# Where one weight tile's conversion stands at the end of the first block, and where the next batch's loads stand in the load queue

## Chip, cores and metric

The kernel runs on one core of a Trainium2 chip. Its time is the device time of one execution in microseconds; several executions are timed, and the median is given. One more execution was recorded by the hardware profiler: the profile and the trace are of that one.

## What is computed

Two stages follow each other. The first is a linear attention for 8 batches of 8 heads, each with 576 rows of 64 values: `kv = k^T v`, `out = q kv`, then each row of `out` is divided by its root mean square and multiplied by `g_norm`. The result is laid out as x, 4608 rows (tokens) of 512. The second stage is `h = x w_in` (512 to 2048), `g = max(0.01 h, h)`, and the output `g w_out` (2048 to 512), in float32. The two weights arrive as 64-bit floats and are converted to 32-bit in the kernel.

```python
def _attn_ref(q, k, v, g_norm):
    kv = np.einsum('bhsd,bhse->bhde', k, v)
    out = np.einsum('bhsd,bhde->bhse', q, kv)
    rms = np.sqrt(np.mean(out * out, axis=-1, keepdims=True) + 1e-06)
    return (out / rms * g_norm).astype(np.float32)

def _moe_ref(x, w_in, w_out):
    h = x @ w_in
    g = np.maximum(0.01 * h, h)
    return (g @ w_out).astype(np.float32)
```

## The kernel before

**Blocks and units.** The 4608 tokens are cut into nine blocks of 512. Block 0 is computed in the ordinary way by `first_block` with three of the four chunks of the weights, while the rest of the weights is still on its way. Block 1, the remainder of block 0 and the other blocks then run in the main loop, by a scheme of seven products in place of eight (Strassen's, in Winograd's form): `product_h` makes h, `product_o` makes the output. Blocks 2 and later use the scheme twice over for h (`product_h_two`). A unit is one chunk of one block. Units are numbered by `now`; each has seven slots `t`, one per product, and `at = 7 * now + t` counts slots from the start of the main loop. The output's products of a unit follow two slots behind its h (`LAG`).

**Converting a weight tile.** A tile is 128 x 512 values, and there are 32. `round_f64` converts one with two steps on ScalarE (ACT: `add` L264 and `cut` L262, reading the raw 64-bit tile), one on VectorE (DVE, L266), one on ACT (L271), and two on VectorE (L281, L284). `round_w(j)` begins tile j: it does L264, L262 and L266. `finish_w()` does the other three of a tile that was begun. The raw tiles share a few buffers, so the load of tile 28 waits until tile 25's two first ACT steps have read theirs.

**Block 0.** `first_block` runs n from 0 to 12. Step n makes one piece of h (eight h_ps matmul records), lets ACT turn it into g (L1143), and then makes the output products of the piece before it (eight o_acc records), which need that g. `between(n, 0)` is called ahead of these output products and `between(n, 1)` behind them. What they do stands in `plan`: a number begins that tile, `f` finishes the one begun, `a` and `t` do a step of the attention for batch 1 or the rest of batch 0, and `x` makes the sums of x for block 1. The last lines are

```python
(8, 1): (21, f, a), (9, 0): (a, a, a, a, a, a, 22, f), (9, 1): (x, 23),
(10, 0): (f, 24), (10, 1): (f, 25), (11, 0): (f,)}
```

At n = 11 the last piece of h is made, and at n = 12 its output products. Behind them ACT (L1156) and VectorE (L1158) copy the block's four sums out of PSUM. In this part of the program each engine's order is the order in which the code issues instructions (`pin`).

**The first slots of block 1.** `product_h` works in pairs of PSUM banks (h_a and h_c, then h_b and h_d). The products go into the banks in the order h_a, h_c, h_a, h_c, h_a, h_c, h_a; each is read by ACT (`copy`, L938, L940, L945) or added by VectorE (L698) before the next one goes into the same bank.

**Sums of weights.** POOL (GpSimd) makes sums and differences of weight quarters for the products of the scheme, and `combine` makes more, in the buffer `stage`, for the double scheme. `put_off` and `write_later` write them to DRAM some slots later (L735, in the profile w<-w_all, w<-stage and w<-pairs), so that `stage` can be used again; from slot 26 on `read` (L822, w_all<-w) fetches them in the order of use. POOL also makes sums of g (`gs`) for the output's products, and sums of x in `stage` for block 2.

**Loads of the attention's inputs.** `to_load` is a list of small load jobs: the k and v tiles of a pair of heads (two transfers, L138) or its q tile (four transfers, L168). The attention's steps append to it, and one job is taken at the end of each slot:

```python
load_some(2 if at in (19, 20) else 1)
```

All of these, the writes and the reads are issued by one engine, SP, in the order of the code. Output stores are issued by ACT (L1114). Each transfer of SP and ACT increments one of eight completion semaphores, taken in turn by the scheduler, and is preceded by a wait for the last transfer that used that semaphore.

Of the kernel before, what the change touches and what calls it, by code (L numbers as in the profile page):

```python
# [24 lines left out]
def kernel(  # L25
# [121 lines left out]
    def load_some(n=1):  # L147

        while to_load and n > 0:
            b, p, what = to_load.popleft()  # L150
            load_pair(b, p, what)
            n -= 1

    def load_pair(b, p, what="kvq", homes=None):


        if "k" in what:
            for i, (to, src) in enumerate(((k_ins, k), (v_ins, v))):
                to[b, p] = load_two(nc.sync, src[b, 2 * p:2 * p + 2],
                                    homes[i] if homes else in_tile("kv"[i]))  # L160
        if "q" not in what:
            return
        t = homes[2] if homes else ins.tile([P, T * D], F32, tag="q_in", name="q_in")
        for l in range(2):
            for c in range(2):
                r0, n = 64 * l + 32 * c, T * D - 32 * c
                src = q[b, 2 * p + half_of(p, l)].rearrange("(t s) d -> t (s d)", s=T)
                pin(nc.sync.dma_start(t[r0:r0 + 32, :n], src[:, 32 * c:]))  # L168
        q_ins[b, p] = t
# [132 lines left out]
    def load_w(j, *eng):  # L302
        eng = eng or (nc.sync,)
        dst, src = w_jobs[j]
        if w_in.dtype == I64:
            w_raws[j] = load_f64(src.bitcast(U32), eng)
        else:
            load(dst, src, eng)

    def rounding(j, high_first=False):  # L310
        if w_in.dtype == I64:
            yield from round_f64(w_jobs[j][0], w_raws.pop(j), high_first)
# [418 lines left out]
    def write_later():  # L731
        for item in list(later):
            item[0] -= 1
            if item[0] < 0:
                pin(nc.sync.dma_start(*item[1:]))  # L735
                later.remove(item)
# [81 lines left out]
    def read(to):  # L818
        nonlocal n_read
        while n_read < min(to, len(reads)):  # L820
            c, k = reads[n_read]
            pin(nc.sync.dma_start(w_place(n_read), w1_dram[c][:, SLOT[k], :, :]))  # L822
            n_read += 1
# [140 lines left out]
    def inner_w2(c):  # L964
        y = w2_sb[1][c]
        t1, t2, t3, t4 = (w2_sb[0][c][:, u, N2 + s * P:N2 + s * P + P]
                          for u in range(2) for s in range(2))
        y11, y12, y21, y22 = (y[:, u, s * P:s * P + P] for u in range(2) for s in range(2))
        add(nc.gpsimd, t1, y12, y11, True)
        add(nc.gpsimd, t2, y22, t1, True)  # L970
        add(nc.gpsimd, t3, y22, y12, True)
        add(nc.gpsimd, t4, y21, t2, True)

    def inner_g(n, half):

        g = g_of(n)[3]
        a11, a21, a12, a22 = (g[:, n, :] for n in range(4))
        s1, s2, s3, s4 = (gi[:, n, :] for n in range(4))
        if half == 0:
            add(nc.gpsimd, s1, a21, a22)  # L980
            add(nc.gpsimd, s2, s1, a11, True)
        else:
            add(nc.gpsimd, s3, a11, a21, True)
            add(nc.gpsimd, s4, a12, s2, True)
# [115 lines left out]
    def go(steps, n=None):  # L1100
        while n is None or n > 0:
            if next(steps, steps) is steps:
                return
            n = None if n is None else n - 1
# [13 lines left out]
    def load_part(os, key):  # L1118

        os[key] = opool.tile([P, 2, N2], F32, tag="o", name=f"o{key}", bufs=6)  # L1120
        r0, c0 = ((int(d) - 1) * N2 for d in key)
        pin(nc.sync.dma_start(
            os[key], part_dram[r0:r0 + N2, c0:c0 + N2].rearrange("(t p) m -> p t m", p=P)))

    def first_block(between):
# [27 lines left out]
        for t in range(4):  # L1153
# [9 lines left out]
    t, a, f, x = "tafx"  # L1163
# [2 lines left out]
            (5, 0): (13, f, a), (5, 1): (14, f), (6, 0): (15, f), (6, 1): (16, f),  # L1166
            (7, 0): (a, a, 17, f), (7, 1): (a, 18, f), (8, 0): (19, f, a, 20, f),
            (8, 1): (21, f, a), (9, 0): (a, a, a, a, a, a, 22, f), (9, 1): (x, 23),
            (10, 0): (f, 24), (10, 1): (f, 25), (11, 0): (f,)}
    loaded, x_sides = 12, None  # L1170

    def between(n, half):
# [56 lines left out]
    def go_o():  # L1229
        while o_queue:  # L1230
            if next(o_queue[0], o_queue) is not o_queue:
                return True
            o_queue.popleft()
# [3 lines left out]
    for i, chunks in rounds:  # L1237
# [7 lines left out]
        for c in chunks:  # L1245
# [5 lines left out]
            for t in range(7):  # L1251
                slot = 7 * c + t
                go(h_steps, 1)
                if not one:

                    if t == 6:
                        go(h_steps, 1)
                    if slot in LATE_SLOTS:
                        go(late, 1)
                    for _ in range(FINE_SLOTS.get(slot, 0)):  # L1260
                        go(a_steps, 1)
                    if i + 1 < NB:
                        if slot == 20:
                            x_sides, new_quarters, sums, inner = sides_x(i + 1)
                        if slot in (20, 21, 22):
                            go(sums, 2 if slot == 20 else 1)
                        if slot == 24:
                            inner(0)
                        elif slot == 25:
                            inner(1)  # L1270
                    load_some()

                if now - 1 in seconds:
                    for half in range(2):
                        if t == (6 if half else 4):
                            inner_g(now - 1, half)
                    if t == 5 and now - 1 < 2 * NC + NC - K:
                        inner_w2(units[now - 1][1])
                if (7 * now + t == 7 * NC + 4):
                    while writes:  # L1280
                        pin(nc.sync.dma_start(*writes.pop()))
                if slot in HELD and i == NB - 1:
                    pass
                elif waited == LAG:
                    go_o()
                elif o_queue:
                    waited += 1
                write_later()
                at = 7 * now + t
                for key in PARTS.get(at, ()):  # L1290
                    if at == 33:
                        part_os = os
                    load_part(part_os, key)
                if at in READS:
                    read(READS[at])
                if one:
                    if not rest and rounded < len(w_jobs):
                        steps = rounding(rounded)
                        rest.extend((3, 3, 1))
                        rounded += 1  # L1300
                    if rest:
                        go(steps, rest.popleft())
                    if loaded < min(rounded + 2, len(w_jobs)):
                        load_w(loaded)
                        loaded += 1
                    for chunk, only in DIRECT.get(at, ()):
                        go(combine(chunk, 2, only=only))
                    if at == 18:
                        direct_0 = combine(0, 2, nc.vector)
                    if at in (18, 19, 22, 23):  # L1310
                        go(direct_0, 1)
                    if t == 3 and nxt[0] < 2 and nxt[1] != c:
                        h_sides, more_h = sides_w1(nxt[1])
                        if now == 0:
                            go(combine(0, 1))
                    if t == 5 and nxt[0] < 2 and nxt[1] != c:
                        more_h()
                    if t == 0 and units[now - 1][1] != c and now > 0:
                        for part in range(2):
                            go(combine(c, part))  # L1320
                    if at in (15, 16):
                        load_pair(2, at - 15)
                    go(late, LATE_ONE.get(at, 0))
                    go(a_steps, A_SLOTS.get(at, 0))
                    load_some(2 if at in (19, 20) else 1)
                    if at == 7 * NC - 4:
                        x_sides, _, sums, _ = sides_x(0)
                    elif at == 7 * N1 - 4:
                        x_sides, new_quarters, sums, inner = sides_x(2)
                    if at in (7 * NC - 4, 7 * NC - 3, 7 * N1 - 4, 7 * N1 - 3):  # L1330
                        go(sums, 2)
                    if at == 7 * N1 - 3:
                        inner(0)
                    elif at == 7 * N1 - 2:
                        inner(1)
# [44 lines left out]
```

## Time and profile before

| | us |
|---|---|
| median of 3 runs | 923.47 (921.96 to 923.55) |
| profiled execution, its own time | 920.04 |
| its span in the profile | 918.3 |
| TensorE (PE) busy in the span | 906.4 |
| VectorE (DVE) busy | 621.1 |
| ScalarE (ACT) busy | 346.9 |
| GpSimd (POOL) busy | 391.0 |
| the profile's mean DMA rate | 220 GB/s |

Times in the profile are microseconds from the start of the span. Between the span and the execution's time lie 1.7 us. The three timed runs lie 1.9 to 3.5 us above the profiled execution. In a timeline a row gives start, duration, engine, line and operation, output and inputs by name, shape, and in brackets the time that the engine was idle just before and what ended that. L126 and L698 are helpers for matmuls and for additions, so their rows are told apart by the tiles. PE is TensorE's matmul, PEld its weight load, SPq the queue of SP.

### The profile page before, as it was taken

The numbers are of one execution on the slowest core, as the hardware profiler recorded it, in microseconds if no ns is written. First come the engines' busy times: TensorE is split into PE (matmuls) and PEld (weight loads), VectorE is DVE, ScalarE is ACT, GpSimd is POOL, SyncE is SP. The second block draws the span as 40 slices with busy tenths as digits, with TensorE's granted clock in tenths as the row PEclk, the third lists the DMA queues.
The fourth block names the chain that finished last, engine by engine and source line by source line (L and its number), as shares of the span: only waits on it lengthen the run. The fifth ranks groups of instructions, "written<-read, shape, count | busy, mean of one in ns | idle before, by whom it ended". The sixth has DMA issues, their size and how long they took to land.

```text
span 918.3 us, 18139 instructions
## 1 busy us (share of the span) xinstructions
PE 906.4 (99%) x7024; PEld 783.8 (85%) x7024; DVE 621.1 (68%) x1127; ACT 346.9 (38%) x679; POOL 391.0 (43%) x467
## 2 busy tenths in 40 slices
PE   8999899999999999999999999999999999999998
PEld 4544388878898999899999999999999999999997
DVE  5765855767556876687756876578669755755565
ACT  5756464132235233433243334332443333223330
POOL 2000479969633473226421642264226522542222
PEclk9999999999999999999999999999999999999999
DMA  8998175897989778777886788758765676666633
GB/s 261 223 270 210 60 242 172 231 307 220 340 280 317 222 226 260 232 234 216 247 261 218 233 247 268 224 168 207 251 180 175 188 221 199 181 194 218 200 108 92
DMA packets 92405, 202.16 MB, mean 220 GB/s; under 512 B 10016, under 2 KB 44448, under 8 KB 92320
## 3 DMA queue, kind: packets, MB, share of 16 engines
q1 hardware_dynamic: 81344, 189.14, 69.3%
q10 hardware_dynamic: 10528, 10.69, 3.5%
q8 instruction: 56, 0.92, 0.4%
q0 software_dynamic: 448, 1.18, 0.3%
q14 instruction: 29, 0.24, 0.1%
HBM read 173.44 MB, written 27.53 MB: 219 GB/s over the span
## 4 chain that ended last, share of the span: by engine, by line
PE 88%; DVE 4%; DMA 3%; ACT 2%; issue 1%; SPq 1%; POOL 1%; DVEq 0%; ACTq 0%; POOLq 0%
PE o_c L126 18%; PE o_a L126 18%; PE h_ha L126 11%; PE h_hb L126 10%; PE h_hc L126 8%; PE h_hd L126 8%; PE h_ps L126 3%; PE o_acc L126 3%; PE o_ps L126 3%; PE h_a L126 1%; PE h_c L126 1%; DMA pairs<-in_v_dram 1%; PE kv_ps L126 1%; PE h_b L126 1%; DMA w_all<-w 1%
## 5 line engine op out<-in xcount | busy, mean ns | idle before, releaser
L698 POOL TENSOR_TENSOR gs<-g 128x512 f32<-128x512 f32 x66 | 84.8, 1285 | 249.1 <-ACT g L913 249.1
L913 ACT ACTIVATE g<-g 128x512 f32<-128x512 f32 x127 | 80.1, 631 | 146.4 <-DVE g L698 146.3
L1032 ACT COPY w_all<-h_ha 128x512 f32<-128x512 f32 x84 | 48.9, 582 | 170.6 <-PE h_ha L126 158.3
L126 PE MATMUL o_c<-pairs,gs 128*128 128x256 f32 x392 | 93.2, 381 | 0.0
L126 PE MATMUL o_a<-pairs,gs 128*128 128x256 f32 x392 | 93.0, 380 | 0.0
L698 DVE TENSOR_TENSOR o<-h_hb,o 128x128 f32<-128x128 f32 x104 | 29.8, 286 | 83.4 <-ACT pairs L1032 83.3
L126 PEld LDWEIGHTS o_c<-pairs,gs 128*128 128x128 f32 x392 | 71.3, 190 | 9.5 <-POOL pairs L698 1.2
L126 PEld LDWEIGHTS o_a<-pairs,gs 128*128 128x128 f32 x392 | 71.3, 190 | 8.1
L698 DVE TENSOR_TENSOR o<-o_a,o 128x512 f32<-128x512 f32 (+1 forms) x93 | 62.5, 672 | 23.0 <-PE o_a L126 22.5
L698 DVE TENSOR_TENSOR o<-o_c,o 128x512 f32<-128x512 f32 x80 | 54.7, 683 | 26.0 <-PE o_c L126 25.7
L126 PE MATMUL h_ha<-stage,w_all 128*128 128x128 f32 x448 | 59.9, 276 | 0.9 <-POOL stage L698 0.9
L126 PEld LDWEIGHTS h_ha<-stage,w_all 128*128 128x128 f32 x448 | 56.7, 192 | 4.0 <-POOL stage L698 1.1
L698 DVE TENSOR_TENSOR g<-g,pairs 128x512 f32<-128x512 f32 x84 | 55.6, 689 | 1.9
L698 POOL TENSOR_TENSOR pairs<-g 128x128 f32<-128x128 f32 x52 | 23.7, 456 | 77.0 <-PE h_hb L126 48.4
L698 DVE TENSOR_TENSOR w_all<-h_hc,w_all 128x512 f32<-128x512 f32 x56 | 38.3, 684 | 15.8 <-PE h_hc L126 15.8
L698 DVE TENSOR_TENSOR o<-h_hd,o 128x128 f32<-128x128 f32 x78 | 22.1, 283 | 38.1 <-ACT pairs L1032 38.0
L126 PE MATMUL o_acc<-w,g 128*128 128x512 f32 x96 | 43.8, 598 | 3.6 <-ACT g L1143 3.6
L126 PE MATMUL h_hb<-stage,w_all 128*128 128x128 f32 x336 | 46.7, 275 | 0.0
L698 POOL TENSOR_TENSOR gs<-gs,g 128x512 f32<-128x512 f32 x33 | 44.7, 1355 | 2.6
L698 POOL TENSOR_TENSOR gs<-g,gs 128x512 f32<-128x512 f32 x33 | 45.4, 1377 | 0.0
L1032 ACT COPY pairs<-h_hb 128x384 f32<-128x384 f32 x84 | 40.0, 476 | 13.7 <-PE h_hb L126 13.3
L126 PE MATMUL h_hb<-xT,w_all 128*128 128x128 f32 x224 | 43.3, 275 | 0.0
(240 smaller groups left out, 2240.8 us busy)
## 6 DMA issues: line engine op xcount, KB each, us to landing
w_all<-w SPq DMA_DIRECT2D x196, 448.0 KB, 4.2
pairs<-w SPq DMA_DIRECT2D x56, 512.0 KB, 4.4
out_dram<-o ACTq DMA_DIRECT2D x35, 256.0 KB, 4.9
v_in<-in_v_dram SPq DMA_DIRECT2D x27, 288.0 KB, 4.4
k_in<-in_k_dram SPq DMA_DIRECT2D x26, 288.0 KB, 4.2
q_in<-in_q_dram SPq DMA_DIRECT2D x52, 144.0 KB, 5.7
q_in<-in_q_dram SPq DMA_DIRECT2D x52, 140.0 KB, 5.7
w<-stage SPq DMA_DIRECT2D x12, 512.0 KB, 4.1
```

What stands on the lines that cost most here:

```text
L126: pin(nc.tensor.matmul(*args, **kw))
L698: ins = eng.tensor_tensor(out_, a, b_, op=ALU.subtract if minus else ALU.add)
L913: first_turn(nc.scalar.activation(t, t if src is None else src, func=AF.Prelu, alpha=SLOPE))
L1032: nc.scalar.copy(q[:, at], bank)
```

## The change

Two places change. In `plan`, tile 24 is still begun ahead of the output products of step 10, but it is finished, and tile 25 begun, one place later: ahead of the output products of step 11, and so behind L1143 of the last piece of h. Tile 25 is finished behind the output products of step 12, the last ones. In the main loop, two load jobs in place of one are taken at slots 24 and 25.

```diff
-            (10, 0): (f, 24), (10, 1): (f, 25), (11, 0): (f,)}
+            (10, 0): (f, 24), (11, 0): (f, 25), (12, 1): (f,)}
...
-                    load_some(2 if at in (19, 20) else 1)
+                    load_some(2 if at in (19, 20, 24, 25) else 1)
```

In the built program the instructions of PE, DVE and POOL stand in the same order as before. On ACT the last L1143 moves ahead of three steps: L271 of tile 24 and L264 and L262 of tile 25. On SP the order before, from slot 24, was: q of pair 0 of batch 3; three writes of w_0; k and v of pair 0; two reads of w_0; q of pair 1; ten writes of w_1 and w_3; k and v of pair 1; a write of w_3_0 from `pairs`; reads and writes as they follow. After the change it is: q, k and v of pair 0; the three writes of w_0; q, k and v of pair 1; the two reads of w_0; the ten writes; the write from `pairs`; then as before. The last of the ten writes, w_3 from `stage`, now stands where v of pair 1 stood.

## The prediction

> **What bounds the kernel now.** I read the page first (busy times, the 40 slices), then TensorE's waits, then the timelines of PE, ACT and DVE around the first edit and of SP and POOL around the second, and last the chain that ended last.
>
> ```profile
> PE 906.4 (99%) x7024; PEld 783.8 (85%) x7024; DVE 621.1 (68%) x1127; ACT 346.9 (38%) x679; POOL 391.0 (43%) x467
> ...
> PE o_acc L126 <- ACT g L1143: 3.6, 1, 3.6
> PE h_ha L126 <- POOL stage L698: 0.9, 1, 0.9
> PE o_ps L126 <- DVE kv L371: 0.4, 1, 0.4
> PE h_b L126 <- ACT g L938: 0.3, 1, 0.3
> PE h_a L126 <- DVE g L698: 0.3, 1, 0.3
> ```
>
> TensorE works 906.4 of 918.3 us, so only its 12 us of idle time can be won. The waits (columns: us in total, times, longest) name five after the start-up, 5.4 us together. The largest is block 0's last group of output products, held once for 3.6 us by the last activation of h. Why it is late stands in the timeline of ACT (start, duration, what it waited for):
>
> ```profile
> 105.71 0.66 ACT L264 ACTIVATE add<-early 128x512 uint32<-128x512 uint32 x1
> 106.27 0.67 ACT L262 ACTIVATE cut<-early 128x512 f32<-128x512 f32 x1
> 109.93 0.63 ACT L271 ACTIVATE w<-cut 128x512 int32<-128x512 f32 x1 [2.98 <-DVE cut L266]
> 110.47 0.65 ACT L264 ACTIVATE add<-early 128x512 uint32<-128x512 uint32 x1
> 111.03 0.65 ACT L262 ACTIVATE cut<-early 128x512 f32<-128x512 f32 x1
> 111.58 0.58 ACT L1143 ACTIVATE g<-h_ps 128x512 f32<-128x512 f32 x1
> ```
>
> Its input was ready at 104.95 (the eight h_ps matmuls start at 101.35 and last 3.60), but L1143 stands in ACT's order behind tile 24's L271, which waits for VectorE until 109.93, and behind tile 25's two ACT steps. VectorE and the copies of the block's sums come next:
>
> ```profile
> 115.23 0.57 ACT L1156 COPY o<-o_acc 128x512 f32<-128x512 f32 x1
> ...
> 117.65 1.27 DVE L1158 COPY o<-o_acc 128x512 f32<-128x512 f32 x2
> 119.50 0.43 DVE L266 TENSOR_SCALAR cut<-cut 128x512 f32<-128x512 f32 x1 [0.58 <-ACT cut L262]
> 119.84 0.68 DVE L698 TENSOR_TENSOR g<-h_c,g 128x512 f32<-128x512 f32 x1
> ```
>
> From 105.83 to 118.92 VectorE works through tiles 23, 24, 25 and the two copies with no idle but for two hand-overs by ACT of 0.70 each. None of that waits for TensorE. For the second edit:
>
> ```profile
> 197.69 0.45 SPq L138 DMA_DIRECT2D k_in<-in_k_dram  x1
> 211.82 0.49 SPq L138 DMA_DIRECT2D k_in<-in_k_dram  x1
> 220.76 0.35 SPq L138 DMA_DIRECT2D v_in<-in_v_dram  x1
> ...
> 200.28 0.73 POOL L698 TENSOR_TENSOR stage<-w_all 128x256 f32<-128x256 f32 x1 [7.79 <-DVE o L698]
> 215.82 1.86 POOL L698 TENSOR_TENSOR gs<-gs,g 128x512 f32<-128x512 f32 x1
> 231.90 0.73 POOL L698 TENSOR_TENSOR stage<-xT 128x256 f32<-128x256 f32 x1 [3.92 <-DMA w<-stage]
> 233.61 0.73 POOL L698 TENSOR_TENSOR stage<-xT,stage 128x256 f32<-128x256 f32 x1 [0.98 <-DMA w<-stage]
> ```
>
> Batch 3's second v load sat 8.4 us in SP's queue, until a store of block 1's output landed (the store issued at 218.53 and took 2.2). In the built program SP's and ACT's transfers take one of eight completion semaphores in turn, and each waits until the last transfer on its semaphore has landed; this load had drawn that store's. And POOL's work from 200.28 on, which runs without a gap to 227.98, starts when the write w<-stage of 256 KB, issued at 197.20, has landed (2.9 us for such a write there); the "DVE o" in its bracket had long been done.
>
> **What the Trainium skill says.** "PSUM — Partial Sum Buffer", Terms: TensorE writing and ScalarE or VectorE reading one bank at once is an error. So a product waits until the bank's last content was read: here the fourth product (h_c, 120.93) begins 0.4 after the add of 119.84 ended. "SBUF — State Buffer", Who interferes with whom: a VectorE instruction with two SBUF inputs contends with a GpSimd one that reads SBUF. The trace agrees: the custom add L284 took 0.68 at 104.12 with POOL idle and 1.64 at 106.85 with POOL at work. "DMA: Bandwidth & Descriptors", Anatomy of one DMA: a semaphore is waited for on the issuing sequencer, before dispatch; so a waiting load holds all behind it, as the 8.4 us show. Same page, Issuing engines are not separate DMA queues: all queues share 16 engines and interleave. From 228 to 236 the stretches show a DMA share of 1.02 to 1.12, so a transfer put ahead delays those behind it.
>
> **Part 1, tile 25 behind the last activation.** Nothing is added or removed. In the built order only ACT changes: L1143 moves ahead of tile 24's L271 and tile 25's L264 and L262; DVE, POOL and SP's loads of tiles stand as before. L1143 then runs at 106.9 (behind tile 24's L262, 106.27 + 0.67) and ends at 107.5, before the o_acc group ahead of it ends (104.94 + 3.67 = 108.61). The 3.6 us are gone: **+3.60**. Tile 25's L264 and L262 follow L271 at 110.47 as now, so VectorE is no later, but no earlier either. Ending tile 25 behind the last product costs nothing for the same reason: VectorE is what its steps wait for.
>
> What is late next? TensorE now reaches block 1 at 112.1 instead of 115.75, but the readers of its banks do not move. The third product (h_a, 119.21 now; it would come at 115.6) waits for the copy of the first, which on ACT stands behind the two L1156: 115.23 + 0.57 + 0.59 + 0.58 gives 117.0. **-1.4**. The fourth (120.93 now; then at 118.7) waits for the VectorE add of the second, behind the two L1158 (to 118.92): L266 and the add took 1.02 from 119.50 to 120.52, so they end at 119.9 and the product starts at 119.95. **-1.25**. Left: 120.93 - 119.95 = 0.98. After it the chain over ACT and VectorE shifts as a whole.
>
> From here to 194 TensorE has 1 us or more in hand everywhere. At 194.77 it waits 0.44 for the copies of kv, at the end of 5.8 us of unbroken VectorE work which starts at 189.09 with a landed write. The DMA share was about 1.0 from 168 to 195, and POOL (one row of work from 132.40 to 192.48, started by a landing) gates some of the writes, so not all of this moves along: I take 0.8 of the 0.98, bounds 0 and 0.98. **-0.2**.
>
> **Part 2, two loads per slot.** Same transfers, other places on SP: the k and v loads of pair 0 pass the three writes of slot 25; pair 1's four q loads and k and v pass the two reads of slot 26, and k and v ten writes too. Buffers are free (their readers on PE ended at 190.7, on DVE at 194.0), so the loads do not wait themselves. What they pass waits:
> - The write that releases POOL at 200.28 stands behind 576 KB of k and v. In the trace these two landed 2.0 us after that write (198.20 + 3.8 against 197.20 + 2.9, by the DMA view); it is 1.6 if they move at 365 GB/s, which the stretches from 189 to 193 show. Some of it fills a gap (share 0.58 in 195 to 196). I take POOL 1.5 later, bounds 0.8 and 2.0. POOL's gs ends at 217.68, TensorE needs it at 219.32: 1.64 in hand, less the 0.8 that TensorE is earlier. **-0.7**, bounds 0 and -1.3.
> - The 0.30 that h_a waits at 224.96 is VectorE's work, which starts from a product ahead of that stall and so keeps its lead: it vanishes. **+0.3**.
> - The 8.4 us of SP do not vanish: the write of w_3 from stage draws the store's semaphore instead of v_in, at the same place in the order, and the burst behind it starts with the store as before (0.8 earlier).
> - In that burst the semaphores shift by one. The write of 229.30, which POOL awaits at 233.61, no longer waits for the second read (issued 222.1, landed 229.24) but for the first (issued 221.64, 6.5 us, 228.15). With the 0.8, POOL is done about 1.4 earlier, and the 0.88 wait at 237.38 goes. **+0.9**, bounds 0 and 0.9.
> - On ACT three output stores (229.45 and 233.84) now await writes that land later, by some 1 to 2 us; the copies behind them have 3 us or more in hand (the product needing the first runs at 236). 0.
> - Batch 3's k and v land early, but are used at 239, where TensorE does not wait for them. 0.
>
> **Sum.** 3.60 - 1.4 - 1.25 - 0.2 - 0.7 + 0.3 + 0.9 = about 1.2 us, all of it kept to the end, since behind 238 TensorE shows no wait of 0.3 or more. The profiled execution took 920.04 (span 918.3, 1.7 around it), so it would take 918.8. It ran 3.4 below the median of the three runs, 923.47; on that I predict 923.47 - 1.2 = 922.3.
>
> **The rivals.**
> - The 3.6 us hold. For it: no other wait is near that size. Against: the two copies end at 118.92 whatever TensorE does. It would need VectorE to be quicker with POOL at its side. 923.47 - 3.6 = 919.9, or with the 1.9 us of smaller waits gone but the 0.98 limit kept, 920.6. Chance 0.15.
> - The lead is used up: POOL's row and the saturated transfers keep 194.77 where it is, or the stalls at 219 and 237 stay. For it: the last chain runs there through q_in, w<-pairs, w_all<-w and w<-stage. About 923.4. This is also what a change without effect gives. Chance 0.22.
> - Slower: the k and v loads, and the q loads behind them, hold POOL's start. It decides when POOL comes more than 2.8 us later: 1.64 are in hand at 219 by today's times, and the stalls of 0.30 and 0.88 behind it absorb 1.2. At 6 us, if all 1,144 KB of k, v and q landed first at some 195 GB/s (the stretches from 177 to 178 and 181 to 182, with q loads under way), TensorE would be 6 - 2.8 = 3.2 later than now: 926.7. Against: the write is issued before those q loads. Chance 0.08.
> - The likeliest, 1.2 us off: 0.55.
>
> **How the numbers follow.** A measurement of this kernel can tell about 0.2% (1.85 us) from no change; the runs shown spread over 1.6. The likeliest lies within, with a spread of 1 us around it: a quarter of it passes 1.85. With nearly all of the first rival that makes faster 0.3, slower 0.09 and same 0.61. The range takes in the first rival's smaller value and the bounds of the likeliest: 920.2 to 924.4.
>
> **What would show it.** Right: no wait of o_acc for L1143; the third and fourth products at about 117.0 and 119.95 with waits of about 1.3 each for ACT's L938 and VectorE's L698; POOL's stage<-w_all near 201.8 and a wait of o_c for POOL's gs near 219; no wait of h_ha for POOL's stage; an SP wait of 8 us on w<-stage, not v_in. Wrong: VectorE's L1158 copies well before 117.6, or a POOL start before 200 or after 203.

## The result and the profile after

| | us |
|---|---|
| before, median of 7 runs | 923.47 (921.16 to 924.17) |
| changed, median of 7 runs | 918.96 (918.58 to 919.86) |
| ratio, with its 95% interval | 0.9957 (0.9945 to 0.9969) |
| profiled execution: before, changed | 920.04, 918.98 |

The changed kernel is 4.5 us faster by the medians, 2.9 to 5.1 us by the interval, where 1.2 was predicted. The two profiled executions lie only 1.06 us apart, close to the 1.2 of the sum. So the sum met the pair of profiles and missed the pair of medians: the difference lies in what the kernel before usually does and did not do in the profile that was read.

The waits of TensorE in the profile after (us in total, times, longest), under the line of busy times:

```profile
PE 906.7 (99%) x7024; PEld 783.6 (85%) x7024; DVE 620.2 (68%) x1127; ACT 347.3 (38%) x679; POOL 391.9 (43%) x467
...
PE h_c L126 <- DVE g L698: 1.6, 1, 1.6
PE h_a L126 <- POOL stage L698: 1.1, 1, 1.1
PE o_ps L126 <- DVE kv L371: 0.9, 1, 0.9
```

The 3.6 us for L1143 are gone, and two waits stand in their place, as predicted. The wait of h_ha for POOL's stage is gone too. The timeline of TensorE shows the two new waits at the third and the fourth product of block 1; the bracket of the third names POOL, but what came last is ACT's copy L938 (116.08 to 116.68):

```profile
112.04 1.89 PE L126 MATMUL h_a<-xT,w_all 128*128 128x256 f32 x8
113.76 1.89 PE L126 MATMUL h_c<-xT,w_all 128*128 128x256 f32 x8
116.77 1.97 PE L126 MATMUL h_a<-xt,pairs 128*128 128x256 f32 x8 [1.12 <-POOL stage L698]
120.38 1.99 PE L126 MATMUL h_c<-xt,pairs 128*128 128x256 f32 x8 [1.65 <-DVE g L698]
```

The timeline of ACT has L1143 where the prediction put it, and that of VectorE shows why the fourth product came 0.43 later than predicted: L266 took 0.97 here, where the profile before had 0.43. POOL was at work beside both. Here L266 began in the middle of a POOL addition (118.19 to 119.45) and ended 0.28 behind it; in the profile before it began where one POOL addition ended and the next began (119.50). That it waits for the addition under way fits this, but was not tested.

```profile
106.74 0.57 ACT L1143 ACTIVATE g<-h_ps 128x512 f32<-128x512 f32 x1
...
117.56 1.27 DVE L1158 COPY o<-o_acc 128x512 f32<-128x512 f32 x2
118.76 0.97 DVE L266 TENSOR_SCALAR cut<-cut 128x512 f32<-128x512 f32 x1
```

For the second edit, POOL starts at 202.36 in place of 200.28, SP stands on a write of w from stage and no longer on v_in, and POOL's sums of x come 0.65 and 1.14 us earlier than before (231.90 and 233.61 there):

```profile
202.36 0.73 POOL L698 TENSOR_TENSOR stage<-w_all 128x256 f32<-128x256 f32 x1 [9.88 <-DMA w<-stage]
...
220.79 0.36 SPq L735 DMA_DIRECT2D w<-stage  x1
...
231.25 0.82 POOL L698 TENSOR_TENSOR stage<-xT 128x256 f32<-128x256 f32 x1 [1.67 <-DMA w<-stage]
232.47 0.73 POOL L698 TENSOR_TENSOR stage<-xT,stage 128x256 f32<-128x256 f32 x1 [0.40 <-DMA w<-stage]
```

### The profile page after: what moved, and what is told of

It reads as the page before. It is cut to its first block, busy times and chain, and to the rows that moved or that the text cites. A ratio compares the mean times of both kernels' runs of the same rounds, so it can differ in the third digit from the quotient of the medians.

```text
span 917.2 us, 18136 instructions
## 1 busy us (share of the span) xinstructions
PE 906.7 (99%) x7024; PEld 783.6 (85%) x7024; DVE 620.2 (68%) x1127; ACT 347.3 (38%) x679; POOL 391.9 (43%) x467
## 3 DMA queue, kind: packets, MB, share of 16 engines
q0 software_dynamic: 448, 1.18, 0.3%
## 4 chain that ended last, share of the span: by engine, by line
PE 82%; DVE 3%; issue 1%; ACT 1%; SPq 1%; DMA 0%; ACTq 0%; DVEq 0%
PE o_c L126 19%; PE o_a L126 18%; PE h_ha L126 11%; PE h_hb L126 11%; PE h_hc L126 8%; PE h_hd L126 8%; PE o_ps L126 3%; PE h_a L126 1%; PE h_c L126 1%; PE h_b L126 1%; DVE g L698 1%; PE h_d L126 1%; PE kv_ps L126 1%; DVE xt L698 0%; DVE o L698 0%
## 5 line engine op out<-in xcount | busy, mean ns | idle before, releaser
L126 PE MATMUL h_ha<-xT,w_all 128*128 128x128 f32 x224 | 43.3, 275 | 0.2 <-ACT g L913 0.2
```

The costliest lines, as they stand in the source:

```text
L126: pin(nc.tensor.matmul(*args, **kw))
```

## The experiments

Each kernel was timed beside the kernel before on the same chip; ratios are to those runs. Theory A: the missing 3.4 us (median before less its profiled execution) are lost between 195 and 240, and part 2 brings the gain. Theory B: they belong to part 1, because VectorE, POOL or ACT are earlier in the usual execution. "Part 1" is the edit of the plan, "part 2" that of the load slots.

**Part 1 alone.** Only the two lines of `plan` from the change's diff.

> Part 1 alone: tile 25 behind the last activation, loads as before. Its profile should show no wait of o_acc for L1143, the third and fourth products at about 116.8 and 120.4, as the changed kernel's does, and the stall of 0.4 at 194.8 gone up to 0.9, so TensorE is no earlier than before from 195 on: a span within 0.5 of before's 918.3. Theory A (the 3.4 us by which the kernel before ran above its profiled execution are lost between 195 and 240, in the chain of loads, writes and POOL that part 2 changes): timed runs at 922 to 924, spread over 3 us as before's. Theory B (they belong to part 1: in the usual execution VectorE is earlier than in the profiled one, and most of the 3.6 us hold): timed runs at 919 to 920, with little spread.

Measured: 920.61 (919.47 to 924.14, 22 runs), ratio 0.9970 (0.9959 to 0.9980). Most of the gain is here, so A falls. The profiled execution was the slowest of the 22 (924.14), its span 4.0 above that of before and not within 0.5; the reason is given with the waits of h_ha below.

**Part 2 alone.** Only the line of `load_some` from the change's diff.

> Part 2 alone: two load jobs per slot at 24 and 25, the plan as before. Its profile should keep the wait of 3.6 of o_acc for L1143, and have no wait of h_ha for POOL near 237. Theory A (the usual execution of before loses its extra 3 us between 195 and 240): timed runs at 918.5 to 920 with a spread near 1 us, part 1 being nearly without effect. Theory B (part 1 brings it): timed runs at 922.5 to 924, spread as before's.

Measured: 922.45 (920.85 to 924.99, 22 runs), ratio 0.9989 (0.9978 to 0.9999). Its profile kept the wait for L1143 (3.87) and had none of h_ha for POOL.

**The kernel before again.** No edit.

> The kernel before, unchanged, under another name: another profiled execution of the same program, and a comparison of it with itself. If the profiled execution of 920.04 was a lucky one of a program that varies, this one's profile is likely to lie nearer to 923.5, and to show in its waits of TensorE where the 3 us go: theory A expects them between 195 and 240 (h_ha for POOL's stage, kv_ps for a load, or gs), theory B none there but a longer wait ahead of block 1. If the profiler itself makes the program quicker, it again lies near 920 while the timed runs lie at 923. The ratio should hold 1.

Measured: 923.39 (921.41 to 927.63, 12 runs), ratio 1.0002 (0.9986 to 1.0019); profiled execution 922.12. Its profile settles where to look. The table of stretches gives the busy time of each engine, PEclk, DMA share and GB/s. First the kernel before as first profiled, then this second profile:

```profile
core 0: us, PE busy (x) PEld busy (x) DVE busy (x) ACT busy (x) POOL busy (x), PEclk, DMA share, GB/s
...
112.00:114.00 2.00, 1.78 (x4) 0.87 (x5) 2.00 (x2) 0.16 (x1) 1.92 (x2) 1.00 0.62 158
114.00:116.00 2.00, 2.00 (x7) 0.98 (x6) 1.30 (x2) 1.15 (x3) 1.92 (x4) 1.00 0.39 105
```

```profile
112.00:114.00 2.00, 1.54 (x2) 0.84 (x3) 2.00 (x2) 0.40 (x1) 1.92 (x2) 0.55 0.44 130
114.00:116.00 2.00, 2.00 (x4) 0.83 (x3) 1.30 (x2) 0.63 (x1) 1.92 (x3) 0.59 0.56 132
```

The same program, the same stall, but in the second one TensorE's granted clock is about half behind the stall, and four matmul records fit into two microseconds that held seven. VectorE's column is the same in both and the wait for L1143 is no shorter (3.86 against 3.60), so B's reason falls: no engine is earlier. This is **theory C**: the stall ahead of block 0's last products costs not only its 3.6 to 3.9 us but, in most executions, a stretch at half clock behind it.

**Half of part 2.**

```diff
-                    load_some(2 if at in (19, 20) else 1)
+                    load_some(2 if at in (19, 20, 24) else 1)
```

> Half of part 2: two load jobs at slot 24 only, so that k and v of pair 0 go ahead of the three writes of w_0 and q of pair 1 goes a slot earlier, while k and v of pair 1 still stand between the reads of slot 26 and the ten writes. The plan is as before. Theory A with the semaphore (what counts is which transfer draws the completion semaphore of the output store): v of pair 1 is no longer there, a write draws it, as in the changed kernel, so the time should be within 1 us of part 2 alone. If what counts is k and v of pair 1 ahead of the two reads, the time stays near 923. Theory B: 923 whatever is done to the loads.

Measured: 922.27 (920.52 to 925.64, 22 runs), ratio 0.9985 (0.9974 to 0.9995): not to be told from the whole of part 2. SP stood on w<-stage at 224, as in the changed kernel, so k and v of pair 1 ahead of the two reads are not what counts. Whether the semaphore or the earlier k and v of pair 0 does was not separated.

**Filling the stall.** Three matmuls, whose result nobody reads, keep TensorE at work; the old plan and loads stay.

```diff
+            if n == 2 * K * U:
+                idle = ps_m.tile([P, NT], F32, tag="ha", name="idle_ps")
+                for _ in range(3):
+                    matmul(idle, lhsT=zeros[:, :P], rhs=zeros[:, :NT], start=True, stop=True)
             between(n, 0)
```

> The kernel before, with three more matmuls of 128 x 512 (each two records, 0.92 us by the o_acc rows, 2.75 us in all) into an unused PSUM bank between the last h_ps group's predecessor o_acc group and the o_acc group that waits 3.6 to 3.9 us for L1143. Nothing is taken away; the wait for L1143 ends when it did. Theory C (the clock: in most executions the idle stretch of 3.6 to 3.9 us makes the chip halve TensorE's granted clock for the o_acc group behind it, as in the profiles of part 2 alone, half of part 2 and the second look at before, where the group took 1.8 to 3.4 us longer; the profiled execution of before escaped it): the added work makes the kernel faster, by 2 to 3 us, to 920.5 to 921.5, with no granted clock below 1 between 110 and 118. Theory B (VectorE, POOL or ACT are earlier in the usual execution, and the 3.6 us hold): no difference, 923.5. If the fill delays what follows: slower by up to 1.

Measured: 922.61 (919.67 to 925.27, 14 runs), ratio 0.9991 (0.9976 to 1.0006). A miss: no gain that can be told. In its profile the clock stayed at 1 and the o_acc group ran at full speed (3.70), as C says, but near 237 h_ha waited 2.0 us for POOL, and of what was won ahead 1.1 was lost there.

**Filling the stall, with part 2.** Both edits; part 2 removes that wait at 237.

> The three matmuls in the stall and part 2, the plan as before. Theory C: the clock's 2 to 3 us and part 2's 1.1 are different losses and add up: 919.5 to 920.5, so about 1 us above the changed kernel (918.96), which is what part 1 brings beside the clock (0.5 to 1.0 us of lead behind the fourth product). If part 2's gain of 1.1 was itself a matter of the clock at that place, no more than 921.

Measured: 920.02 (918.34 to 922.12, 13 runs), ratio 0.9968 (0.9957 to 0.9979). Against part 2 alone (0.9989), work that is added makes the kernel about 1.9 us faster by the ratios (the two were timed beside different runs of before, so the ratios are the fairer measure; their intervals barely overlap). Its timeline of TensorE and its clock in the group:

```profile
109.57 2.74 PE L126 MATMUL idle_ps<-g 128*128 128x512 f32 x6
113.60 3.70 PE L126 MATMUL o_acc<-w,g 128*128 128x512 f32 x8 [1.30 <-ACT g L1143]
...
114.00:116.00 2.00, 2.00 (x6) 0.90 (x5) 2.00 (x2) 0.00 (x0) 1.92 (x3) 1.00 0.81 225
```

The wait for L1143 ends no earlier by this; the only thing that the fill can remove is the half clock. The changed kernel (0.9957, and 0.9962 below) is another 0.6 to 1.0 us faster by the ratios; that would be the rest of part 1, but the intervals overlap.

**Half the plan.** L1143 passes tile 25's two ACT steps only, so that a wait of 2.5 us remains.

```diff
-            (10, 0): (f, 24), (10, 1): (f, 25), (11, 0): (f,)}
+            (10, 0): (f, 24), (10, 1): (f,), (11, 0): (25, f)}
```

> The plan of before with tile 24 finished where it was and tile 25 begun and finished behind the last activation: L1143 passes only tile 25's two ACT steps, so o_acc's wait shrinks from 3.6 to 3.9 by 1.1 to about 2.6, in place of going. Theory C (clock): the stall no longer fills the stretch that halves the clock, so the time falls by its 1.1 and by most of the 2 to 3 us of the half clock, to 919.5 to 921, level with part 1 alone (920.6), though less than a third of the wait is removed. Without the clock, a shorter wait by 1.1 brings 1.0 at most: 922.5.

Measured: 922.47 (918.94 to 926.18, 22 runs), ratio 0.9987 (0.9976 to 0.9999). A miss: the clock was expected to stay up, and in the profile it fell behind 2.5 us of waiting as it had behind 3.6.

```profile
112.00:114.00 2.00, 2.00 (x4) 0.86 (x3) 2.00 (x2) 0.18 (x1) 1.92 (x2) 0.56 0.31 83
```

**Half the plan, with part 2.**

> The half plan (tile 25 begun and finished behind the last activation, tile 24 where it was: a stall of 2.5 us remains) with part 2, which takes away the wait of h_ha near 237 that hid gains ahead of it. Theory C: if a stall of 2.5 us makes the clock halve as often as one of 3.6 to 3.9, the time is about 922.4 (part 2 alone) less 1.1, 921.3; if it does so in some executions only, the runs split into two groups, near 919 and near 921 to 922; if never, 919.2 to 919.8, at or below the 920.0 of the filled stall with part 2. The half plan's one profile had the clock at 0.56 to 0.59 from 112 to 116, so the middle answer is expected.

Measured: 921.07 (918.25 to 923.23, 22 runs), ratio 0.9979 (0.9970 to 0.9988). Its profiled execution (919.64) kept full clock behind its 2.5 us. The median is near the 921.3 of the first answer, with the runs spread over 5 us; sorted by their granted clock, they split in two, as the middle answer had it (below).

**The plan with half of part 2.**

> The changed plan with two load jobs at slot 24 only: the best of the parts so far. If the gains of part 2 come from what draws the store's completion semaphore (now the write of w_3 from stage, in half of part 2 as in the whole), the time is that of the changed kernel, 918.5 to 919.5, and SP stands on w<-stage near 221. If k and v of pair 1 ahead of the two reads matter, it lies between part 1 alone and the changed kernel, 919.5 to 920.5. A version better than the changed kernel would lie at 918.3 or less.

Measured: 919.32 (918.57 to 920.14, 5 runs), ratio 0.9959 (0.9943 to 0.9975): as the changed kernel, not better. o_c waited 0.8 for POOL's gs near 220, the loss that the prediction feared of part 2.

**Copies later.** The changed kernel with VectorE's two L1158 copies two slots into block 1.

```diff
-                in_turn(nc.vector.tensor_copy(o, accs[t]))
+                held.append((t, o, accs[t]))
...
+                if at == 2:
+                    for row, o, acc in held:
+                        pin(nc.vector.tensor_copy(o, acc))
+                        put_off(part_dram[row * P:(row + 1) * P, :], o)
```

> The changed kernel with VectorE's two L1158 copies of block 0's sums issued two slots into block 1, behind the L698 add that the fourth product waits for (their writes to DRAM follow later too). In the changed kernel's profile the fourth product waited 1.65 us for that add, which stood behind 1.27 us of copies; so it should start near 119.1 in place of 120.38. If TensorE's lead at that point is kept to the end, the time is 917.7; if it is used up at 192 to 195, where every kernel with a lead or without one loses 0 to 0.9 us to VectorE's o and kv work, it is the changed kernel's, 918.9; if the later writes of the sums or the later tile 26 delay POOL, up to 920.

Measured: 918.63 (917.52 to 919.64, 6 runs), ratio 0.9955 (0.9938 to 0.9971). The fourth product came at 119.43, 0.95 earlier than in the changed kernel, but at 208 the lead over it was 0.41, and at 219 o_c waited 0.8 for gs. The overlap of the runs with those of the changed kernel is too large to call it better.

**The changed kernel again.**

> The changed kernel, unchanged, under another name: more timed runs beside those of the kernels sent with it, and a second profile. All theories: 918.6 to 919.5 with a spread near 1.5 us; a profile without a granted clock below 1 between 104 and 245, and without a wait of h_ha for POOL near 237.

Measured: 919.10 (918.81 to 919.97, 6 runs), ratio 0.9962 (0.9948 to 0.9977); profiled 918.91, with full clock and the waits of the first profile.

**Three more profiles of the kernel before, one of part 1 alone.** These are single executions with a profile.

> A third profiled execution of the kernel before, to count how often the stall of 3.6 to 3.9 us ahead of the last o_acc group is followed by a granted clock of half. Theory C: in most executions; the o_acc group then takes 1.5 to 3 us longer than the 3.67 of the first profile, TensorE is 2 to 3.5 us later than there at 208, and the execution takes 922 to 924. If the clock is not the main part, the group takes 3.7 and the 2 to 3 us are lost elsewhere.

> A fourth profiled execution of the kernel before, for the same count and with the same expectation as the third.

> A fifth profiled execution of the kernel before, for the same count and with the same expectation as the third.

> A second profiled execution of part 1 alone, whose first (924.14) was the slowest of its 22 runs (median 920.61). A usual one should show no half clock at 112 to 118, TensorE within 0.5 us of the changed kernel at 208, a wait of h_ha for POOL's stage of 1.5 to 2.1 us near 237, no half clock behind it, and take 920 to 921. If the half clock behind the h_ha wait is usual, it takes 922 or more again.

Measured: 922.20, 922.11 and 922.38 for before, 919.59 for part 1. One more execution of before, timed beside these, took 919.69 with a mean granted clock of 1.00; its trace is not kept. Part 1 alone waited 0.4 for POOL at h_ha and not the expected 1.5 to 2.1, and had no half clock. The third profile of before, in its timeline and its stretches:

```profile
112.15 6.37 PE L126 MATMUL o_acc<-w,g 128*128 128x512 f32 x8 [3.61 <-ACT g L1143]
```

```profile
110.00:112.00 2.00, 0.00 (x0) 0.00 (x0) 1.44 (x2) 2.00 (x4) 2.00 (x2) 0.68 0.04 14
114.00:116.00 2.00, 2.00 (x4) 0.94 (x3) 1.30 (x2) 0.66 (x2) 1.92 (x4) 0.50 0.38 96
```

The wait is 3.61 as in the first profile; the group behind it took 6.37 where it had taken 3.70, and the clock was already down in the idle stretch.

All profiled executions side by side. "Group" is the time from the start to the end of the last eight o_acc records; the other columns say how much later TensorE starts the same instruction than in the first profile of before (its time there in the heading; for the last two columns this is a record in the middle of the product), all from the traces.

| execution | us | group | h_a, 115.8 | h_c, 120.9 | h_c, 207.9 | kv_ps, 239.6 |
|---|---|---|---|---|---|---|
| before, 1st | 920.04 | 3.70 | 0 | 0 | 0 | 0 |
| before, 2nd | 922.12 | 5.26 | +1.80 | +1.80 | +2.13 | +2.02 |
| before, 3rd | 922.20 | 6.37 | +2.60 | +2.60 | +2.93 | +2.11 |
| before, 4th | 922.11 | 5.40 | +2.10 | +2.10 | +2.75 | +1.79 |
| before, 5th | 922.38 | 5.40 | +1.64 | +1.64 | +1.70 | +2.27 |
| part 2 alone | 921.51 | 5.28 | +2.51 | +2.51 | +2.84 | +1.50 |
| half of part 2 | 921.84 | 6.67 | +2.86 | +2.86 | +3.21 | +1.81 |
| half the plan | 922.45 | 5.40 | +0.58 | +0.78 | +1.84 | +2.44 |
| half the plan, part 2 | 919.64 | 3.70 | -0.03 | +0.65 | +1.11 | -0.36 |
| filled | 922.58 | 3.70 | +0.42 | +1.20 | +1.44 | +2.54 |
| filled, part 2 | 921.99 | 3.70 | +1.39 | +2.17 | +3.17 | +1.89 |
| part 1 alone, 1st | 924.14 | - | -2.28 | +0.88 | +1.41 | +3.91 |
| part 1 alone, 2nd | 919.59 | - | -3.76 | -0.60 | -0.06 | -0.51 |
| changed, 1st | 918.98 | - | -3.72 | -0.55 | -0.01 | -1.13 |
| changed, 2nd | 918.91 | - | -3.64 | -0.47 | +0.01 | -1.18 |

(Some were late at 104.9 already, ahead of the edit: the first profile of part 1 alone, the filled stall with part 2 and half the plan with part 2 by 1.1, part 2 alone by 0.7, the fourth profile of before and the filled stall by 0.4.) Six of the seven executions with the whole stall ran its group wholly or in part at half clock, four of the five of before among them. Between the last two columns every kernel with part 2 gains 1.1 to 1.5 us (the plan with half of part 2 and the copies later, which waited for gs and are not in the table, 0.4), while the kernels with the old loads go from 1.0 gained to 2.5 lost.

**The clock of all timed runs.** The mean granted clock of each timed run is on record as well. In the traces a stretch of half clock lasts 3.41 us, and one such stretch lowers the mean over 920 us by 0.0019. So it shows: the fourth and the fifth profile of before, with one stretch, have a mean of 0.998, the third, with two, 0.996. The table counts the runs by this and gives the median of each group in us; the waits are those of the profiles.

| kernel, timed runs | wait ahead of the group | full clock (0.999 or 1.00) | one stretch (0.998) | two or more (0.996 or less) |
|---|---|---|---|---|
| before, 136 | 3.6 to 3.9 | 12: 920.9 | 56: 922.8 | 68: 924.1 |
| part 2 alone and half of part 2, 44 | 3.9 | 0 | 26: 921.6 | 18: 922.8 |
| half the plan, 22 | 2.5 | 5: 919.6 | 15: 922.6 | 2: 925.6 |
| half the plan, part 2, 22 | 2.5 | 6: 919.5 | 15: 921.2 | 1: 922.0 |
| filled, 14 | 1.0 | 13: 922.6 | 1: 925.3 | 0 |
| filled, part 2, 13 | 1.3 | 13: 920.0 | 0 | 0 |
| part 1 alone, 22 | 0.3 or none | 20: 920.5 | 2: 924.0 | 0 |
| changed, 13 | none | 13: 919.0 | 0 | 0 |

The kernel before again had at least one stretch in all of its 12 runs, the plan with half of part 2 and the copies later had none in their 11. So what theory C says does not rest on a few profiles: with the stall, half clock is the usual case, and with the stall filled, 26 of 27 runs kept full clock. The runs of half the plan with part 2 split cleanly: the six at full clock took 918.25 to 920.01, the other sixteen 920.35 to 923.23. Runs within a row are sorted by what happened in them, not by an edit, and where in a timed run its stretches lay is not on record.

## Why the prediction was wrong, point by point

**Where it failed.** The step is the last one, "on that I predict 923.47 - 1.2 = 922.3", and under it the term **+3.60**: the stall was priced at its own length, from a profile with a granted clock of 1.00 throughout, and the sum of that execution was carried over to the median. In the usual execution of before the stall costs its 3.6 to 3.9 us and then 1.6 to 2.7 us in the o_acc group (5.26 to 6.37 against 3.70). Removing the stall removes both. At the first h_a product (115.8) the four other profiles of before are 1.64 to 2.60 later than the first, less 0.4 in one that started so much later; the changed kernel is 3.6 to 3.7 earlier. So part 1 brings 5.3 to 6.3 us there, not 3.6, and behind the two new waits some 2.1 to 3.1 remain. The first profile was a rare case: 12 of 136 timed runs of before kept full clock, and of 143 (919.18 to 929.04) five lie under 920.5. The clock of the runs also splits the gain: of the 4.5 us, about 2.4 lie between all runs of before (median 923.3) and those at full clock (920.9), and about 2 between these and the changed kernel (919.0). That the three timed runs then shown lay 1.9 to 3.5 above it was in the text, and was taken as an offset that the change keeps, when it was a loss that the change could remove.

**What was luck.** That the 1.2 of the sum is so near the 1.06 between the two profiles is so in part by errors that cancel. The sum gave part 1 a gain of 0.75 (3.60 - 1.4 - 1.25 - 0.2) and part 2 one of 0.5 (-0.7 + 0.3 + 0.9); in these two profiles the first ended as 0.0 at 194.8, and the second brought 1.1.

**What the Trainium skill has on it.** The section "Part 1: The HAM clock gate" of "TensorE: Matmul & The Clock Gate" says that the clock is cut to half after about one idle window of 3.4 us and given back after a busy one, and that these windows run freely, so that the moment varies. The prediction did not use it. The traces agree with the window: worked out from stretches of 0.5 us, the half clock lasted 3.41 us in six of the eight executions that had it near 112 or 240, and 6.83 us, twice that, in the other two, the third profile of before and half of part 2. Its onset varied with the execution, 2.2 to 4.1 us after the last product ahead of the stall had ended. That one wait of 3.60 was not followed by half clock would fit windows that run freely. What does not fit an idle window of 3.4 us is that shorter waits, one of 2.48 us (half the plan) and one of 2.06 us (below), were followed by it too.

**Part 1's other terms.** "-1.4" and "-1.25": right in kind; the third product came at 116.77 (117.0 predicted), the fourth at 120.38 (119.95), so 0.55 was left and not 0.98, by the 0.97 of L266. That a product waits for its bank's last reader shows better here than in the profile before, where TensorE was busy until 120.93 anyway: the add ended at 120.33, the fourth product began at 120.38. (And POOL was not quite idle beside the L284 of 104.12: a copy of one value ran from 104.42.) "-0.2": it was all of it; at 194.76 o_ps waited 0.9 and TensorE stood where it had stood before (194.77).

**Part 2.** "-0.7": POOL came 2.08 later (1.5 taken, 2.0 the bound), but since its operations ran shorter (gs 1.27, before 1.86), gs ended at 219.40 and cost TensorE 0.2 there; in two other kernels with early loads TensorE waited 0.8 for it. "+0.3" and "+0.9": both waits went. SP waited 1.5 for the reads of weights in place of 5.8, which fits the path that was described; with the loss at gs taken off, 1.1 us are left from 208 on. By the ratios part 2 is worth 1.0 us on the kernel before (interval 0.1 to 2.0) and 1.2 on top of part 1, which cannot be told apart. The h_ha wait, 0.88 in the first profile, was absent in the third profile of before, 0.3 in the fourth, 1.3 in the second and 2.0 in the fifth, the one of these four whose TensorE came earliest; and in the first profile of part 1 alone the half clock followed it too:

```profile
239.92 1.32 PE L126 MATMUL h_ha<-stage,w_all 128*128 128x128 f32 x6 [2.06 <-POOL stage L698]
```

```profile
240.00:242.00 2.00, 2.00 (x11) 2.00 (x12) 0.00 (x0) 0.59 (x1) 1.92 (x4) 0.58 1.05 354
```

That cost it another 1.4 us against the filled stall, which came as early and waited as long there (2.5 lost between the last two columns, against 1.1). It is the slowest of its 22 runs.

**The rivals.** "The 3.6 us hold" named nearly the measured time (919.9) by a wrong reason: VectorE was not quicker, and the two waits took most of its 3.6. "The lead is used up" came true for part 1 in the pair of profiles (TensorE at 194.76 against 194.77), but the stall at 237 went, and the time was not 923.4. Slower did not happen.

**What stays open.** The four later profiles of before took 922.1 to 922.4, the median of its timed runs is 923.3. Part of this may be a second stretch of half clock, which half of the timed runs had (median 924.1) and three of these four profiles had not; but the third, which had it, took 922.2 as well. A second stretch does not need the wait of h_ha, since part 2 alone and half of part 2, without that wait in their profiles, had it in 18 of 44 runs. What the runs with one stretch (922.8) have above the profiles with one (922.1 to 922.4) is not explained. Nor is the filled stall without part 2: at full clock it took 922.6, the kernel before at full clock 920.9. Its one profile shows 1.1 of that lost near 237. And at full clock, too, runs of one kernel differ, those of part 1 alone by up to 4.6 us.

## What to carry to other kernels

A stall of TensorE of 2.5 us or more, as here, is to be priced at its length plus a likely stretch of half clock behind it, even where the profile at hand shows full clock: one execution tells nothing about how often the clock falls. The mean granted clock of each timed run does tell it, without a trace. When the profiled execution lies below all timed runs, ask which wait could cost more in the others before taking the difference as a constant. And test two edits together as well as apart: the fill brought 0.8 us alone, within its error, and about 2 once the later wait that swallowed it was gone.

## What the runs showed of the hardware

Matmuls whose result nobody reads made a kernel faster, by keeping TensorE's clock up: the ratio was 0.9968 with them and 0.9989 without. The half clock came in units of 3.41 us, one or two in a trace; of two, 1.4 us already fell into the idle stretch (third profile of before: from 110.72, the products from 112.15). No length of the wait decides it: 2.06, 2.5 and 3.6 us were each followed by it in one execution and not in another. But the longer the wait, the oftener it came: in kernels with part 2 or half of it, which have no wait of h_ha for POOL, half clock came in 44 of 44 runs with a wait of 3.9 us, in 16 of 22 with 2.5, and in none of 13 with 1.3.
